# A Fourier mixer and a long convolution on one core: three kinds of short matmul blocks put together, and another choice of buffers and DMA-split tiles

## The chip, the core and the metric

The kernel runs on one core of a Trainium2 chip. The metric is the device time of one execution in microseconds; the kernel before took 584.09 us as the median of three runs (583.81 to 584.11). The core has five engines with a queue of their own: TensorE (PE, with the weight loads shown apart as PEld), VectorE (DVE), ScalarE (ACT), GpSimd (POOL) and SyncE (SP). Each engine takes its instructions strictly in the order in which the program lists them. Here POOL and SP only issue DMAs.

## What is computed

Two independent results stand side by side in the output:

```python
def _A_ref(x, dft_seq_re, dft_seq_im, dft_hid_re, dft_hid_im):
    a = jnp.einsum("bsd,ed->bse", x, dft_hid_re)
    b = jnp.einsum("bsd,ed->bse", x, dft_hid_im)
    return jnp.einsum("ts,bse->bte", dft_seq_re, a) - jnp.einsum("ts,bse->bte", dft_seq_im, b)

def _B_ref(u, log_A_real, A_imag, C_real, C_imag, log_dt, D_skip):
    dt = jnp.exp(log_dt)
    A = -jnp.exp(log_A_real) + 1j * A_imag
    C = (C_real + 1j * C_imag) * dt[:, None]
    P = jnp.exp((A * dt[:, None])[:, :, None] * jnp.arange(L)[None, None, :])
    K = 2.0 * jnp.einsum("dn,dnl->dl", C, P).real          # 512 channels, 128 states, 2048 taps
    y = irfft(rfft(u.T, 2 * L) * rfft(K, 2 * L), 2 * L)[:, :L].T
    return y + u * D_skip

return jnp.concatenate([_A_ref(...), _B_ref(...)], axis=-1)   # 2048 rows, 512 + 512 columns
```

All is float32. `x` and `u` have 2048 rows and 512 columns.

## The kernel before

**The first half, called the stream here.** The Fourier mixer is two chains of large matmuls (class `Fnet`). The sequence matrices S come in 8 groups (4 column blocks, real and imaginary), each of 16 tiles of 128x512; then 4 groups of 8 tiles take the results `p` back from DRAM and multiply them by the hidden matrices. To get float32 precision from the fast fp32r matmul, each tile is split into `hi` and `lo`, and each product is three matmuls (hi x hi, hi x lo, lo x hi) of 128x512 into one of four PSUM banks `acc`: 640 such triples, all at L366. A split takes one ACT instruction (L221, hi) and one DVE instruction (L225, lo), from a buffer `raw` that SP's DMA filled. There is a second way (`load_soft`): POOL issues a DMA that casts S to `hi`, ACT writes -hi into `lo` (L318), and a second DMA of POOL adds S onto it; DVE has no part in it. The table `SOFTS` says which tiles go this way: 28, four in each of groups 1 to 7. `RAWS` = 7 raw buffers and `DEPTH` = 4 pairs hi/lo hold what is ahead of PE.

**The second half, called the blocks.** The convolution (class `Ssm`) is a hand-made Fourier transform in small matmuls, each kind a block of PE work put between matmuls of the stream. All blocks write two PSUM buffers `f` of two banks each, handed out by `banks`:

- `stage1_u` (L890, 8 blocks): first step of the transform of u; results go out through ACT and two DVE instructions (L902, L904) for each buffer.
- `taps` (L801, 16 blocks): the convolution's taps K from two tables t1 and t2 that DVE builds by repeated products (L605, L614, L628, L634). This is most of DVE's work.
- `stage1_k` (L832, 8 blocks): first step of the transform of K.
- `product` (L992, 16 blocks, four in each of four quarters of the channels): second step of both transforms; ACT copies the result (L1006) and DVE forms the complex product (L1009, L1011, L1019, L1022).
- the inverse's first step, tile name `ia` (L1029, 16 blocks, four in each quarter), and its last step, tile name `ib` (L1078, 8 blocks, two in each quarter).

**What sets the order.** Nothing is scheduled on the chip. Python generators describe the work; each yields the engine, an assumed duration and an urgency, and the class `Plan` runs them like a small event simulation on the host and writes the instructions down in the order that comes out. For PE a yield also names the number of instructions, since `Plan.fetched` assumes that they are loaded in pieces of 256. So a change of an assumed duration or of a table moves instructions on every engine. `LATE` gives the urgency of the products of each quarter, `JOIN` the number of quarters whose `ia` may be put into the same block as a `taps` (class `Joined`, list `waiting`); before, `JOIN` is 0 and none is.

Of the kernel before, what the change touches and what calls it, by code (L numbers as in the profile page):

```python
# [11 lines left out]
AF = mybir.ActivationFunctionType  # L12
# [42 lines left out]
APART = None, True  # L55
LATE = 1, 1, 3, 1


def HELD():
    return 1  # L60


# [20 lines left out]
class Plan:  # L83
# [103 lines left out]
def dve(cols, rate=1.0):  # L187
    return (66 + cols / rate) / 960
# [6 lines left out]
class Fnet:  # L195
# [149 lines left out]
    def matmuls(self):  # L345
        nc = self.nc
        for g in self.groups:
            still = (self.x, self.x_ev) if g[0] == "s" else (self.w, self.w_ev)
            items, acc = self.items[g], []
            for batch in [[i] for i in items[:-BATCH]] + [items[-BATCH:]]:  # L350
                for d in range(4):
# [3 lines left out]
                    for i in batch:  # L355
# [53 lines left out]
class Joined(Event):  # L409
# [18 lines left out]
class Ssm:  # L428


    def __init__(self, tc, ctx, plan, fnet, nd, ldt, dsk, uG, f1u, f1k, w2, ia, ib, out):
# [14 lines left out]
        self.t1s, self.t2s, self.css = Sem(2), Sem(1), Sem(2)  # L446
        self.kss, self.res, self.xks = Sem(1), Sem(1), Sem(1)
        self.waiting, self.taps_left, self.pars = [], 16, Sem(1)
        self.sets, self.set_ev = {}, [Event(), Event()]
# [27 lines left out]
    def banks(self, n):  # L477
# [7 lines left out]
        self.plan.put(self.one)  # L485
        return got

    def give(self, k):
# [294 lines left out]
    def taps(self, ks, n, done):  # L783
# [4 lines left out]
        other = self.waiting.pop(0) if self.waiting else None  # L788
        got = yield from self.banks(2 if other else 1)
        k, p = got[0]  # L790
        yield "pe", 1.97 + (1.05 if other else 0), None, 320 if other else 256
        if other:
            other.run(got)
        t1, t2 = self.t1.pop(n), self.t2
# [13 lines left out]
        while self.waiting and not self.taps_left:  # L808
# [3 lines left out]
                             p[:, :, 256:].rearrange("p o (i l) -> p l o i", i=4), AF.Copy)  # L812
        if other:
            other.leave(k)
        else:
            self.give(k)
        done()

    def stage1_k(self, ks, n, ev):
# [6 lines left out]
        got = yield from self.banks(2)  # L826
        yield "pe", 1.11, None, 64
        for a in range(2):
# [50 lines left out]
    def stage1_u(self, k):  # L879
# [4 lines left out]
        got = yield from self.banks(2)  # L884
        yield "pe", 1.13, None, 32
        for r in range(2):
# [94 lines left out]
    def product(self, b, h, q, got, done):  # L981
# [22 lines left out]
        def half(r, k, p):  # L1004
            yield "act", act(1024), HELD
            a.activation(uk[:, r].rearrange("p g c n d -> p g (c n d)"), p, AF.Copy)  # L1006
            self.give(k)
            yield "dve", dve(512)
            v.tensor_tensor(P[:, r], t[:, r], u[:, r], op=OP.mult)  # L1009
            yield "dve", dve(512), *APART  # L1010
            v.tensor_tensor(t[:, r], t[:, r], u[:, r, :, ::-1], op=OP.mult)  # L1011
            left[0] -= 1
            if not left[0]:
                self.plan.set(ready)
        for r in range(2):
            self.plan.spawn(half(r, *got[r]), LATE[h])
        yield ready
        yield "dve", dve(512)
        v.tensor_tensor(u[:, :, :, 0], P[:, :, :, 0], P[:, :, :, 1], op=OP.subtract)  # L1019
# [3 lines left out]

        def run(got):
            for c, Y in enumerate((u, t)):
# [41 lines left out]
    def inverse(self, b, h, i, n):  # L1067
# [8 lines left out]
        for w in range(n // 2):  # L1076
            for y in range(2):
                nc.tensor.matmul(ps[64 * y:64 * y + 64, w // 4, PART * (w % 4):PART * (w % 4) + PART],  # L1078
                                 self.ib[:, n * i + 2 * w + y], z[:, 2 * w + y], start=True, stop=True,
                                 tile_position=(0, 64 * y))  # L1080
        o = n * i // 2
        for w in range(0, n // 2, 4):
            yield "act", act(512)
            nc.scalar.activation(z[:, w:w + 4], ps[:, w // 4].rearrange("p (w d) -> p w d", w=4), AF.Copy)
        self.give(k)
        yield "dma", load(32 * n, 270)
# [81 lines left out]
```

## Time and profile before

| what | value |
|---|---|
| median of three runs | 584.09 us |
| the profiled execution's own time | 582.56 us |
| its span, first to last instruction | 580.8 us |
| TensorE clock granted | 0.999 |
| PE blocks of the convolution by line | L890 8, L801 16, L832 8, L992 16, L1029 16, L1078 8 |
| DMA moved | 133.10 MB |

The profile gives each engine's busy time, the chain of work that ended last, groups of instructions by line, and a timeline. A matmul's row lasts longer than the distance to the next row's start, because matmuls overlap; what a block costs is read from the starts. The records count an fp32 matmul of a block twice and an fp32r matmul of the stream once, and each has a weight load beside it.

### The profile page before, as it was taken

The page shows a single profiled execution, that of the slowest core. Times are in us where ns is not written, and L with a number is a line of the kernel's source. Part 1 is how long each engine was busy: PE and PEld are TensorE (multiplying, and loading weights), DVE is VectorE, ACT ScalarE, POOL GpSimd, SP SyncE. Part 2 cuts the span into 40 slices and gives each one's busy share as a digit, 9 for nine tenths or more (in the row PEclk, how much of TensorE's full clock was granted, in tenths as well). Part 3 has the DMA queues.
Part 4 walks back from the last instruction along what each step waited for, and adds up shares of the span by engine and source line. Part 5 has one row for each costly group of instructions (what it writes and reads, how often), then busy time and mean ns, then how long its engine had stood idle before and what let it go on. Part 6 is the DMA issues. An engine that isn't in the chain of part 4 may idle for free.

```text
span 580.8 us, 15376 instructions
## 1 busy us (share of the span) xinstructions
PE 571.1 (98%) x6150; PEld 436.1 (75%) x6150; DVE 512.5 (88%) x911; ACT 371.2 (64%) x729; POOL 40.3 (7%) x60
## 2 busy tenths in 40 slices
PE   8999999999999999999999999999999999999996
PEld 6877777788777777778877777777687777776685
DVE  6999999999999999999999999999989999346410
ACT  4779665763777595768568585945588744445522
POOL 0000000000100000100000001001100000000000
PEclk9999999999999999999999999999999999999999
DMA  8999999986469767876797887479989995789564
GB/s 248 327 372 263 280 294 276 285 262 170 133 159 239 207 171 218 205 180 207 207 222 190 237 216 226 125 186 296 243 280 262 243 282 184 209 251 303 169 195 144
DMA packets 147831, 133.10 MB, mean 229 GB/s; under 512 B 47280, under 2 KB 107312, under 8 KB 147504
## 3 DMA queue, kind: packets, MB, share of 16 engines
q1 hardware_dynamic: 139408, 117.05, 66.7%
q0 software_dynamic: 8064, 14.68, 12.6%
q8 instruction: 48, 0.79, 0.6%
q10 hardware_dynamic: 288, 0.39, 0.2%
q14 instruction: 23, 0.19, 0.1%
HBM read 89.36 MB, written 42.73 MB: 227 GB/s over the span
## 4 chain that ended last, share of the span: by engine, by line
PE 70%; DVE 23%; issue 4%; DMA 2%; SPq 0%; ACT 0%; DVEq 0%; ACTq 0%
PE acc L366 55%; DVE prod L605 8%; DVE t L614 4%; PE f L992 4%; PE f L801 3%; DVE lo L225 3%; PE f L1029 3%; PE f L1078 2%; PE f L890 2%; DVE t L634 1%; PE f L832 1%; DVE z L1009 1%; DVE cs L675 1%; DMA zl<-zs 1%; DVE uk L1011 1%
## 5 line engine op out<-in xcount | busy, mean ns | idle before, releaser
L366 PE MATMUL acc<-hi,x_hi 128*128 128x512 f32 x640 | 258.2, 403 | 0.3 <-ACT hi L221 0.3
L366 PE MATMUL acc<-lo,x_hi 128*128 128x512 f32 x640 | 250.2, 391 | 0.0
L366 PE MATMUL acc<-hi,x_lo 128*128 128x512 f32 x640 | 249.7, 390 | 0.1
L605 DVE TENSOR_TENSOR prod<-t,cs 128x1024 f32<-128x1024 f32 (+4 forms) x192 | 163.1, 867 | 1.7 <-ACT t L723 0.6
L366 PEld LDWEIGHTS acc<-hi,x_hi 128*128 128x128 f32 x640 | 120.1, 188 | 49.8 <-issue 23.7
L366 PEld LDWEIGHTS acc<-hi,x_lo 128*128 128x128 f32 x640 | 120.3, 188 | 26.5 <-DVE x_lo L225 0.5
L366 PEld LDWEIGHTS acc<-lo,x_hi 128*128 128x128 f32 x640 | 120.3, 188 | 23.0 <-DVE lo L225 0.2
L221 ACT ACTIVATE hi<-raw 128x512 fp32r<-128x512 f32 x132 | 82.6, 627 | 64.0 <-PE acc L366 48.5
L225 DVE TENSOR_TENSOR lo<-raw,hi 128x512 fp32r<-128x512 f32 x132 | 90.1, 684 | 28.2 <-ACT hi L221 21.9
L614 DVE TENSOR_TENSOR t<-prod 128x512 f32<-128x512 f32 (+4 forms) x192 | 94.0, 511 | 1.0
L621 ACT ACTIVATE square<-t 128x256 f32<-128x256 f32 (+1 forms) x64 | 36.7, 573 | 31.0 <-DVE t L614 28.3
L320 POOL DMA_DIRECT2D lo<-in_sT x28 | 24.3, 868 | 214.1 <-ACT lo L318 33.8
L1006 ACT ACTIVATE uk<-f 128x1024 f32<-128x1024 f32 x32 | 31.1, 1017 | 11.8 <-PE f L992 11.8
L801 PEld LDWEIGHTS f<-t,t 128*32 128x32 f32 x2048 | 29.5, 110 | 7.9 <-issue 5.8
L801 PE MATMUL f<-t,t 128*32 128x64 f32 x2048 | 32.4, 220 | 1.9 <-issue 1.4
L389 ACT ACTIVATE y<-acc 128x512 f32<-128x512 f32 x47 | 28.0, 595 | 8.7 <-PE acc L366 8.6
L1009 DVE TENSOR_TENSOR z<-uk 128x512 f32<-128x512 f32 x32 | 21.9, 684 | 9.6 <-ACT uk L1006 7.4
L315 POOL DMA_DIRECT2D hi<-in_sT x28 | 16.2, 577 | 189.4 <-PE acc L366 147.0
L1044 ACT ACTIVATE z<-f 128x512 f32<-128x512 f32 x32 | 17.7, 592 | 13.3 <-PE f L1029 13.3
L634 DVE TENSOR_TENSOR t<-square 128x128 f32<-128x128 f32 (+1 forms) x64 | 24.6, 385 | 0.0
L992 PE MATMUL f<-xt,w 64*32 64x256 f32 x768 | 23.5, 379 | 0.0
L1011 DVE TENSOR_TENSOR uk<-uk 128x512 f32<-128x512 f32 x32 | 22.1, 690 | 0.9
(94 smaller groups left out, 490.7 us busy)
## 6 DMA issues: line engine op xcount, KB each, us to landing
raw<-in_sT SPq DMA_DIRECT2D x99, 256.0 KB, 5.4
p<-y SPq DMA_DIRECT2D x32, 256.0 KB, 3.2
xk<-xk_sb SPq DMA_DIRECT2D x32, 256.0 KB, 5.2
zs<-z SPq DMA_DIRECT2D x32, 256.0 KB, 3.3
zl<-zs SPq DMA_DIRECT2D x16, 512.0 KB, 5.0
raw<-p SPq DMA_DIRECT2D x32, 256.0 KB, 4.4
hi<-in_sT POOLq DMA_DIRECT2D x28, 256.0 KB, 4.6
lo<-in_sT POOLq DMA_DIRECT2D x28, 256.0 KB, 4.9
```

The costliest lines, as they stand in the source:

```text
L221: self.nc.scalar.activation(hi, src, AF.Copy)
L225: self.nc.vector.tensor_tensor(lo, src, hi.bitcast(F32), op=OP.subtract)
L366: nc.tensor.matmul(acc[d], l[:, cols], r, start=k == 0 and n == 0, stop=k == len(items) - 1 and n == 2)
L389: self.nc.scalar.activation(y, ps, AF.Copy, scale=-1.0 if g[2] == 1 else 1.0)
L605: self.nc.vector.tensor_tensor(p.rearrange("p k d c m -> p k (d c) m"), src.rearrange("p d c l -> p (d c) l")[:, None, :, rows].to_broadca ...
L614: self.nc.vector.tensor_tensor(dst[:, :, :, rows], p[:, 0], p[:, 1, :, ::-1], op=OP.add)
L621: self.nc.scalar.activation(sq, t[:, :, :, m // 2:m], AF.Square)
L634: self.nc.vector.tensor_tensor(t[:, :, 0, m:2 * m:2], box[0][:, :, 0], box[0][:, :, 1], op=OP.subtract)
L801: nc.tensor.matmul(ps[32 * j:32 * j + 32, i], t1[:, d, c], t2[:, d, c], start=c == 0, stop=c == 1, tile_position=(0, 32 * j))
L992: nc.tensor.matmul(got[r][1][32 * xx:32 * xx + 32, g, 256 * c:256 * c + 256], self.w2[rows, 2 * q + r, xx, 32 * c:32 * c + 32], xt[rows].r ...
L1006: a.activation(uk[:, r].rearrange("p g c n d -> p g (c n d)"), p, AF.Copy)
L1011: v.tensor_tensor(t[:, r], t[:, r], u[:, r, :, ::-1], op=OP.mult)
```

## The change

Five things change.

1. `JOIN` 0 becomes 2: an `ia` of quarters 0 and 1 waits for the next `taps` and is written into the same block, ahead of it, into the free half of the same buffers. The block then takes both buffers.
2. `WAITS` = 3 is new: an `ib` of quarters 0, 1 and 2 waits in the list `late` for a later `ia` block (or for a `taps` block, where no `ia` waits), and is written into it at columns 256 on. Its result then lies in two buffers.
3. In the products of quarters 0 to 2 the two DVE multiplications, until now made for each half as soon as it was there, are made once for both halves (`times`). `LATE` of quarter 2 goes from 3 to 1, and the urgency of these multiplications in quarter 3 is `LAST`.
4. `SOFTS` takes 30 tiles, five in each of groups 2 to 7; `RAWS` 7 becomes 5 and `DEPTH` 4 becomes 5.
5. Some assumed durations of PE blocks are other numbers, which moves instructions alone.

```diff
-LATE = 1, 1, 3, 1
+LATE = 1, 1, 1, 1
+def LAST():
+    return LATE[3]
...
-                    dur += 0.11 if stream else 0.09
+                    dur += 0.14 if stream else 0.11
...
-                        yield "pe", 0.683, None, 6
+                        yield "pe", 0.681, None, 6
...
 class Joined(Event):
-    def run(self, got, shared=True):
-        self.got, self.users = got, {k: 1 for k, _ in got}
-        if shared:
-            self.users[got[0][0]] = 2
-        self.fn(got)
+    def run(self, got, users, zone=0):
+        self.got, self.users, self.zone = got, users, zone
+        for k, _ in got:
+            users[k] = users.get(k, 0) + 1
+        self.fn(got, zone)
...
+    def ia_done(self):
+        self.ia_left -= 1
+        while len(self.late) > self.ia_left:
+            self.plan.set(self.late.pop(0))
...
     def taps(self, ks, n, done):
         other = self.waiting.pop(0) if self.waiting else None
-        got = yield from self.banks(2 if other else 1)
+        late = self.late.pop(0) if self.late and not other else None
+        got = yield from self.banks(2 if other or late else 1)
...
-        yield "pe", 1.97 + (1.05 if other else 0), None, 320 if other else 256
+        yield "pe", 1.97 + (1.05 if other else IB if late else 0), None, 320 if other or late else 256
...
     def product(self, b, h, q, got, done):
-            yield "dve", dve(512)
-            v.tensor_tensor(P[:, r], t[:, r], u[:, r], op=OP.mult)
-            yield "dve", dve(512), *APART
-            v.tensor_tensor(t[:, r], t[:, r], u[:, r, :, ::-1], op=OP.mult)
+            if h == 3:
+                yield from times(slice(r, r + 1), LAST)
...
+        def times(r, urgency=None):
+            n = 512 * (r.stop - r.start)
+            yield "dve", dve(n), urgency
+            v.tensor_tensor(P[:, r], t[:, r], u[:, r], op=OP.mult)
+            yield "dve", dve(n), urgency, True
+            v.tensor_tensor(t[:, r], t[:, r], u[:, r, :, ::-1], op=OP.mult)
...
         yield ready
+        if h < 3:
+            yield from times(slice(0, 2))
...
         if w.got is None:
+            late = self.late.pop(0) if self.late else None
             got = yield from self.banks(2)
-            yield "pe", 1.05, None, 64
-            w.run(got, False)
+            yield "pe", 1.15 + (IB if late else 0), None, 128 if late else 64
+            users = {}
+            w.run(got, users)
+            if late:
+                late.run(got, users, 256)
+                self.plan.set(late)
+            self.ia_done()
...
     def inverse(self, b, h, i, n):
-        (k, ps), = yield from self.banks(1)
-        yield "pe", 0.14 + 0.11 * n, None, 4 * n
...
+        j = Joined(self, run)
+        if h < WAITS and self.ia_left > len(self.late):
+            self.late.append(j)
+            yield j
+        if j.got is None:
+            got = yield from self.banks(1)
+            yield "pe", IB, None, 64
+            j.run(got, {})
...
-CHUNK, FIRST, JOIN = 32, 128, 0
-RAWS, DEPTH, STAGED, AHEAD = 7, 4, 4, 3
+CHUNK, FIRST, JOIN = 32, 128, 2
+RAWS, DEPTH, STAGED, AHEAD = 5, 5, 4, 3
 ISSUE = 1.0
-SOFTS = {(g, k) for g in range(1, 8) for k in (3, 7, 11, 15)}
+SOFTS = {(g, k) for g in range(2, 8) for k in (2, 5, 8, 11, 14)}
 BATCH = 2
+WAITS = 3
+IB = 0.14 + 0.11 * 16
```

What this does to the order is seen at three places. In the listings L370 is L366 of before, L816 is L801, L1050 is L1029, L1110 is L1078, L916 and L918 are L902 and L904, L615, L624 and L685 are L605, L614 and L675, and L229 is L225.

The first place is PE's queue where quarter 0 begins its inverse. Before, a `taps` block (t tables into `f`), five triples of the stream, and then `ia` alone:

```order
L801 MATMUL f_2315<-t_124,t_1803 32x64 x64
L366 MATMUL acc<-hi,x_hi_309 128x512
...
L366 MATMUL acc<-hi,x_lo_323 128x512
L1029 MATMUL f_2429<-uk,ia 64x256 x2
L1029 MATMUL f_2430<-uk,ia 64x256 x2
...
L366 MATMUL acc<-hi,x_hi_322 128x512
```

Now `ia` stands directly ahead of a later `taps`, in one of its two buffers (f_2619):

```order
L370 MATMUL acc<-hi,x_lo_141 128x512
L1050 MATMUL f_2619<-uk,ia 64x256 x2
L1050 MATMUL f_2620<-uk,ia 64x256 x2
...
L1050 MATMUL f_2620<-uk,ia 64x256 x2
L816 MATMUL f_2619<-t_124,t_2141 32x64 x64
L370 MATMUL acc<-hi,x_hi_140 128x512
L370 MATMUL acc<-lo,x_hi_140 128x512
```

All eight `ia` of quarters 0 and 1 are moved so; the stream has no matmul between the two kinds any more.

The second place is PE's queue at the inverse's last step. Before, `ib` stood between matmuls of the stream:

```order
L366 MATMUL acc<-lo,x_hi_140 128x512
L366 MATMUL acc<-hi,x_lo_141 128x512
L1078 MATMUL f_3412<-zl,ib 64x128 x16
L366 MATMUL acc<-hi,x_hi_140 128x512
L366 MATMUL acc<-lo,x_hi_140 128x512
```

Now it follows an `ia` of quarter 2, in two parts for two buffers:

```order
L370 MATMUL acc<-hi,x_lo_420 128x512
L1050 MATMUL f_5548<-uk,ia 64x256 x2
...
L1050 MATMUL f_5549<-uk,ia 64x256 x2
L1110 MATMUL f_5548<-zl,ib 64x128 x8
L1110 MATMUL f_5549<-zl,ib 64x128 x8
L370 MATMUL acc<-hi,x_hi_419 128x512
```

Five of the eight `ib` are written in this way; the last three stand alone as before. Before, one `ib` happened to follow a `taps` with no stream between them. In all, PE's queue is cut into 60 stretches of the stream now, and into 72 before.

The third place is DVE's queue ahead of the first `taps`. The buffer that the first `taps` takes comes free with one DVE instruction, the second of a `stage1_u` result. Before, that is the last row but one here, and 6 `stage1_u` blocks and 297 matmuls of the stream stand ahead of the first `taps` on PE:

```order
L675 TENSOR_TENSOR cs<-seed 128x704
L225 TENSOR_TENSOR lo<-raw,hi 128x512
...
L605 TENSOR_TENSOR prod<-t_938,cs 128x512
L902 TENSOR_TENSOR zl<-f_930,zl 128x512
L904 TENSOR_TENSOR zl<-f_930,zl 128x512
L654 SCALAR_TENSOR_TENSOR seed<-seed 128x352
```

Now all 8 `stage1_u` blocks and 348 matmuls of the stream stand ahead of it, and the DVE instruction is the third row from the end here:

```order
L615 TENSOR_TENSOR prod<-t_986,cs 128x1024
L229 TENSOR_TENSOR lo<-raw,hi 128x512
L624 TENSOR_TENSOR t_986<-prod 128x32x16
L916 TENSOR_TENSOR z<-f_1056,z 128x512
L918 TENSOR_TENSOR z<-f_1056,z 128x512
L916 TENSOR_TENSOR zl<-f_1113,zl 128x512
L918 TENSOR_TENSOR zl<-f_1113,zl 128x512
```

On DVE 25 instructions more stand ahead of that release than before: 8 splits (L229), 4 pairs of `stage1_u` results (L916 and L918), 3 table products of 1024 columns (L615), 3 sums of 512 and one of 256 columns (L624), and two short ones on the seeds (L664 and L666, which are L654 and L656 of before).

More of the change, by code (lines that the diff above doesn't have):

```diff
@@ L447, in __init__ @@
         self.kss, self.res, self.xks = Sem(1), Sem(1), Sem(1)
+        self.late, self.ia_left = [], 16
         self.waiting, self.taps_left, self.pars = [], 16, Sem(1)
@@ L812, in taps @@
                              p[:, :, 256:].rearrange("p o (i l) -> p l o i", i=4), AF.Copy)
-        if other:
-            other.leave(k)
-        else:
+        users[k] -= 1
+        if not users[k]:
             self.give(k)
@@ L826, in stage1_k @@
         got = yield from self.banks(2)
[L827 removed]
+        yield "pe", 1.06, None, 64
         for a in range(2):
@@ L1073, in inverse, with run @@
             nc.sync.dma_start(z[:, o:o + 8], self.zs[h].rearrange("s c l d -> (s c) l d")[:, n * i + o:n * i + o + 8])
-        (k, ps), = yield from self.banks(1)
-        yield "pe", 0.14 + 0.11 * n, None, 4 * n
[L1076 to L1080, printed above, removed]
-        o = n * i // 2
-        for w in range(0, n // 2, 4):
-            yield "act", act(512)
-            nc.scalar.activation(z[:, w:w + 4], ps[:, w // 4].rearrange("p (w d) -> p w d", w=4), AF.Copy)
-        self.give(k)
+        o = n * i // 2
+        def run(got, zone):
+            for w in range(n // 2):
+                for y in range(2):
+                    if len(got) == 2:
+                        to = got[w // 4][1][64 * y:64 * y + 64, w // 2 % 2, zone + PART * (w % 2):zone + PART * (w % 2 + 1)]
+                    else:
+                        to = got[0][1][64 * y:64 * y + 64, w // 4, PART * (w % 4):PART * (w % 4) + PART]
+                    nc.tensor.matmul(to, self.ib[:, n * i + 2 * w + y], z[:, 2 * w + y], start=True, stop=True,
+                                     tile_position=(0, 64 * y))
+        j = Joined(self, run)
[6 more added lines that the diff above has]
+            j.run(got, {})
+        for m in range(2):
+            yield "act", act(512)
+            to = z[:, 4 * m:4 * m + 4]
+            if len(j.got) == 2:
+                src = j.got[m][1][:, :, j.zone:j.zone + 2 * PART].rearrange("p b (w d) -> p b w d", w=2)
+                to = to.rearrange("p (b w) d -> p b w d", b=2)
+            else:
+                src = j.got[0][1][:, m].rearrange("p (w d) -> p w d", w=4)
+            nc.scalar.activation(to, src, AF.Copy)
+            if len(j.got) == 2:
+                j.leave(j.got[m][0])
+        if len(j.got) == 1:
+            j.leave(j.got[0][0])
         yield "dma", load(32 * n, 270)
```

10 lines of the change are left out of this document (7 added, 3 removed).

## The prediction, as it was put on record

> **What bounds the kernel now.** First the page's head, its busy row and the shares of the chain that ended last:
>
> ```profile
> span 580.8 us, 15376 instructions
> PE 571.1 (98%) x6150; PEld 436.1 (75%) x6150; DVE 512.5 (88%) x911; ACT 371.2 (64%) x729; POOL 40.3 (7%) x60
> PE 70%; DVE 23%; issue 4%; DMA 2%; SPq 0%; ACT 0%; DVEq 0%; ACTq 0%
> ```
>
> PE is busy almost throughout, so time can only come from what PE loses between or inside its blocks. The 23% of DVE in the chain call for a view by stage (columns: stage and length in us, busy time and count of PE, PEld, DVE, ACT and POOL, granted clock, DMA share, GB/s):
>
> ```profile
> 0.00:83.00 83.00, 80.95 (x400) 59.26 (x400) 77.23 (x150) 59.17 (x121) 4.60 (x10) 1.00 0.94 299
> 83.00:490.00 407.00, 404.25 (x4893) 312.61 (x4897) 401.19 (x709) 274.67 (x549) 35.67 (x50) 1.00 0.80 220
> 490.00:580.80 90.80, 85.92 (x873) 64.23 (x862) 34.03 (x54) 37.41 (x60) 0.00 (x0) 0.99 0.69 206
> ```
>
> The reader is to see two full engines up to 490 us: DVE has 401 of 407 us busy in the middle stage. A block put into PE's queue before DVE has its data makes PE wait; the stream's work left over then ends later. After 490 us only PE is full. The granted clock is 1.00, so it explains nothing here.
>
> **Term 1, fewer changes between stream and blocks.** Two places of the timeline, one clean block and the one pair that already stands together (columns: start, duration, engine and line):
>
> ```profile
> 487.86 0.39 PE L366 MATMUL acc<-lo,x_hi 128*128 128x512 f32 x1
> 488.09 0.39 PE L366 MATMUL acc<-hi,x_lo 128*128 128x512 f32 x1
> 488.41 1.99 PE L801 MATMUL f<-t,t 128*32 128x64 f32 x128
> 490.33 0.50 PE L366 MATMUL acc<-hi,x_hi 128*128 128x512 f32 x1
> 490.67 0.40 PE L366 MATMUL acc<-lo,x_hi 128*128 128x512 f32 x1
> ...
> 429.87 1.99 PE L801 MATMUL f<-t,t 128*32 128x64 f32 x128
> 431.79 1.97 PE L1078 MATMUL f<-zl,ib 128*64 128x128 f32 x32
> 433.69 0.50 PE L366 MATMUL acc<-hi,x_hi 128*128 128x512 f32 x1
> ```
>
> In the stream a start follows a start after 0.23 us. Into a block it is 0.32 (488.09 to 488.41), and the first matmul after it holds the next for 0.34 (490.33 to 490.67): 0.09 and 0.11, together 0.20 us for each block that stands alone. The pair without stream between shows that putting together saves all of it: the taps take 1.92 from start to start alone and 1.92 in the pair, and the inverse's last step 1.90. The order has 60 stretches of stream against 72, so 12 x 0.20 = **-2.4 us**. No row shows `ia` directly ahead of taps; the bounds are half the saving (-1.2) and a quarter more (-3.0), and I take the row of the pair.
>
> [...]
>
> **Term 2, the first taps.** The buffer of the first taps comes free with a DVE instruction (L904), and PE waited for it:
>
> ```profile
> 82.52 0.39 PE L366 MATMUL acc<-hi,x_lo 128*128 128x512 f32 x1
> 83.00 1.99 PE L801 MATMUL f<-t,t 128*32 128x64 f32 x128
> ...
> 76.59 0.68 DVE L902 TENSOR_TENSOR zl<-f,zl 128x512 f32<-128x512 f32 x1
> 77.31 0.69 DVE L904 TENSOR_TENSOR zl<-f,zl 128x512 f32<-128x512 f32 x1
> 77.92 0.88 DVE L675 TENSOR_TENSOR cs<-seed 128x704 f32<-128x704 f32 x1
> 82.16 0.69 DVE L904 TENSOR_TENSOR zl<-f,zl 128x512 f32<-128x512 f32 x1
> 82.77 0.52 DVE L654 SCALAR_TENSOR_TENSOR seed<-seed 128x352 f32<-128x352 f32 x1
> 83.20 0.42 DVE L614 TENSOR_TENSOR t<-prod 128x256 f32<-128x256 f32 x1
> 83.54 0.34 DVE L656 TENSOR_SCALAR seed<-seed 128x352 f32<-128x352 f32 x1
> 189.42 1.22 DVE L605 TENSOR_TENSOR prod<-t,cs 128x1024 f32<-128x1024 f32 x1
> 190.56 0.68 DVE L1019 TENSOR_TENSOR uk<-z 128x512 f32<-128x512 f32 x1
> ```
>
> DVE ended at 82.85 and the taps began at 83.00, 0.48 after the last matmul, not 0.32: DVE set this start. The order puts 25 more DVE instructions ahead of this release. By starts of these rows: 8 splits and 3 sums of 512 columns at 0.61 (77.31 to 77.92) are 6.7; 4 pairs L902 and L904 at 1.33 (76.59 to 77.92) 5.3; 3 products of 1024 at 1.14 (189.42 to 190.56) 3.4; the three short ones 0.43 (82.77 to 83.20), 0.34 and, its 0.34 less the overlap of the others, 0.25: 1.0. That is 16.4 us more. PE's way to that place grows by 51 matmuls of the stream and two L890 blocks:
>
> ```profile
> 28.80 1.11 PE L890 MATMUL f<-xt,f1u 32*64 32x512 f32 x16
> 29.84 0.50 PE L366 MATMUL acc<-hi,x_hi 128*128 128x512 f32 x1
> 255.18 17.27 PE acc L366 x75
> ```
>
> At 0.23 (17.27 / 75) these are 11.7, and two blocks at 1.04 and 0.20 are 2.5: 14.2. DVE comes 16.4 - 14.2 = 2.2 us later against PE. Since DVE has some air (77.23 of 83), I take **+2.1 us**, with 0 and 2.5 as bounds. Behind the waiting taps stands all of PE's queue, so this is paid in full.
>
> **Term 3, the later waits for DVE.** After the first taps PE loses at these places:
>
> ```profile
> 154.79 1.10 PE L801 MATMUL f<-t,t 128*32 128x64 f32 x64
> 156.26 1.10 PE L801 MATMUL f<-t,t 128*32 128x64 f32 x64 [0.37 <-DVE t L614]
> 157.29 0.50 PE L366 MATMUL acc<-hi,x_hi 128*128 128x512 f32 x1
> 163.63 1.12 PE L832 MATMUL f<-ks,f1k 32*64 32x256 f32 x32 [0.56 <-DVE ks L824]
> 492.60 1.12 PE L1029 MATMUL f<-uk,ia 32*64 32x256 f32 x32
> L1029 PE MATMUL f<-uk,ia 32*64 32x256 f32 x512 | 20.2, 389 | 0.3
> ```
>
> The taps at 154.79 take 2.50 where 1.92 is clean (0.58); L832 at 163.63 comes after 0.56 idle; the sixteen `ia` have 20.2 us busy against 16 x 1.12 = 17.9, 2.3 in all, which I put down to DVE as well, the last to write their operand. That is 3.4 us. Now `ia` of the first two quarters stands ahead of a taps whose tables DVE makes later than `ia`'s operand, so that wait should end; and the taps stand later in PE's queue than before, with less work on DVE: 24 pairs of 512 columns (1.22) are one of 1024 (1.14), 24 x 0.08 = 1.9, and two splits fewer are 1.2, so 3.1 us of air. I take **-3.3 us**; bounds -1.0 and -3.4. What is late next is `ia`'s result: it waits for its taps, and the inverse's last step follows it later. Its cover is the stream; without it an `ib` of 1.90 us would stand at the end.
>
> **Term 4, PE's instructions.** The largest single stop on PE is none of these:
>
> ```profile
> 405.63 1.81 PE f L801 x118
> 407.43 1.43 issue
> 408.86 0.41 PE f L801 x10
> 408.86 0.25 PEld L801 LDWEIGHTS f<-t,t 128*32 128x32 f32 x10 [1.59 <-issue]
> q8 instruction: 48, 0.79, 0.6%
> ```
>
> PE stops 1.6 us (its weight loads' idle time) within taps and waits for nothing that is shown. The instruction queue has 48 loads, and PE and PEld have 12300 records: 256 for each. Taps hold 256 records in 1.9 us, where the stream takes 256 in 29 (128 matmuls at 0.23). So the next load can come too late in a dense stretch: here PE stood from 407.43 to 408.86, 3.3 us from the taps' start. The eight new blocks hold 64 + 256 = 320 records in 1.05 + 1.92 = 3.0 us, with more than a whole load in each. Before, one of 16 taps stopped. I estimate 2.3 stops in eight: a stop needs the load's edge in the last 64 to 84 records (10 matmuls with their weights were left at 408.86) of 256, 0.25 to 0.33 each. 2.3 x 1.6 = 3.7, less the 1.6 of before: **+2.1 us**. Bounds: no stop at all, -1.6, and all eight, +11.2; one of 16 speaks for the near end.
>
> [...]
>
> **At nothing.** The DMA-split tiles: each of the two more costs POOL and the queues two loads of 256 KB and takes one split from DVE; POOL is 7% busy and the DMA share is 0.80 in that stage. ACT has one instruction a tile either way. RAWS and DEPTH only change how far ahead tiles lie; if that cover failed, a late tile costs up to its landing:
>
> ```profile
> raw<-in_sT SPq DMA_DIRECT2D x99, 256.0 KB, 5.4
> ```
>
> The end is the same, 15 matmuls of the stream behind the last `ib`.
>
> **Sum.** -2.4 + 2.1 - 3.3 + 2.1 = -1.5. The profiled execution took 582.56 (span 580.8 and 1.8 around it), so 581.1 there; the median of the runs is 1.5 above it, and 584.1 - 1.5 = **582.6 us**.
>
> **Rivals.**
>
> - *Instruction loads decide* (slower): four or more of the joined blocks stop, at 1.6 each as at 407.43. From a little over three the gain is gone; five give 8.0 - 1.6 = 6.4 for term 4, and 584.1 - 2.4 + 2.1 - 3.3 + 6.4 = 586.9; four give 585.3. For it: 320 dense records exceed one load. Against: 15 of 16 taps ran through, and so did the 320 records at 429.87. Chance 0.18, at 585.8.
> - *Loads hidden*: term 4 is -1.6, and the time 578.9. For it the same 15 taps. Chance 0.20. [...]
> [...]
> - *DVE stays the bound*: only 1.0 of term 3 goes, 584.9. For it DVE's 401 of 407 us; against it the later places of the taps. Chance 0.08.
> - *The change doesn't join*: the order shows 13 blocks joined; excluded.
>
> **Chances and range.** The forecast has 0.44, with a range of its own of 581.2 to 584.2. A measurement of this kernel tells 0.2% (1.2 us) from no change, so faster means under 582.9. Of the forecast 0.27 lie there and 0.17 within; hidden loads add 0.20 to faster; drain adds 0.10 to no change; DVE splits 0.04 and 0.04; the instruction rival adds 0.02 to no change and 0.16 to slower. Faster 0.47, same 0.33, slower 0.20. The range goes from hidden loads, 578.9, to the instruction rival, 585.8.
>
> **What would show it.** Right: PE's rows with `ia` and taps 2.9 to 3.0 us from first start to the stream and none between; the first taps starting near 99 us with DVE ending just ahead; L1029's successor without waits for L1022 in the first two quarters; two or three pieces of "issue" of 1.5 us inside taps that follow `ia`. Wrong: pieces of "issue" in more than three, PE waiting for hi or lo of the stream (fewer raw buffers), or waits for DVE that come back after 165 us.

## The result: slower by 1.6%

| kernel | median | runs | ratio to before, 95% interval |
|---|---|---|---|
| before | 583.90 us | 582.23 to 584.11 (6 runs) | |
| changed | 593.51 us | 589.27 to 595.10 (6 runs) | 1.0157 (1.0115 to 1.0198) |

The profiled execution of the changed kernel took 589.27 us, the lowest of its six. Where before has runs within 2 us, the changed kernel has them 6 us apart.

### The profile page after: what moved, and what is told of

Its sections match the earlier page's. It is cut to its first block, busy times and chain, and to the rows that moved or that the text cites. A ratio compares the mean times of both kernels' runs of the same rounds, so it can differ in the third digit from the quotient of the medians.

```text
span 587.5 us, 15343 instructions
## 1 busy us (share of the span) xinstructions
PE 572.2 (97%) x6150; PEld 438.0 (75%) x6150; DVE 510.9 (87%) x885; ACT 370.1 (63%) x729; POOL 43.4 (7%) x64
## 4 chain that ended last, share of the span: by engine, by line
PE 85%; DVE 4%; ACT 4%; DMA 3%; issue 2%; SPq 0%; DVEq 0%; ACTq 0%
PE acc L370 67%; PE f L1006 5%; PE f L816 4%; PE f L1110 3%; PE f L1050 3%; PE f L846 2%; DVE prod L615 1%; PE f L904 1%; DVE t L624 1%; DMA xt<-in_uG 1%; DMA par<-par_dram 1%; DMA xu<-zl 1%; ACT L672 1%; ACT L670 1%; ACT hi L225 0%
## 5 line engine op out<-in xcount | busy, mean ns | idle before, releaser
L370 PE MATMUL acc<-hi,x_hi 128*128 128x512 f32 x640 | 257.2, 402 | 0.5 <-ACT y L393 0.4
L370 PE MATMUL acc<-lo,x_hi 128*128 128x512 f32 x640 | 250.5, 391 | 4.4 <-issue 4.4
L370 PE MATMUL acc<-hi,x_lo 128*128 128x512 f32 x640 | 250.3, 391 | 0.0
L615 DVE TENSOR_TENSOR prod<-t,cs 128x1024 f32<-128x1024 f32 (+4 forms) x192 | 164.0, 870 | 3.8 <-ACT t L753 1.4
L370 PEld LDWEIGHTS acc<-hi,x_hi 128*128 128x128 f32 x640 | 120.3, 188 | 46.2 <-issue 19.1
L370 PEld LDWEIGHTS acc<-hi,x_lo 128*128 128x128 f32 x640 | 120.5, 188 | 31.0 <-issue 4.6
L370 PEld LDWEIGHTS acc<-lo,x_hi 128*128 128x128 f32 x640 | 120.5, 188 | 23.6 <-issue 0.3
L225 ACT ACTIVATE hi<-raw 128x512 fp32r<-128x512 f32 x130 | 80.7, 630 | 66.6 <-PE acc L370 56.7
L229 DVE TENSOR_TENSOR lo<-raw,hi 128x512 fp32r<-128x512 f32 x130 | 88.6, 686 | 23.8 <-ACT hi L225 21.8
L624 DVE TENSOR_TENSOR t<-prod 128x512 f32<-128x512 f32 (+4 forms) x192 | 94.9, 512 | 1.1
L324 POOL DMA_DIRECT2D lo<-in_sT x30 | 26.3, 877 | 177.9 <-ACT lo L322 102.1
L816 PEld LDWEIGHTS f<-t,t 128*32 128x32 f32 x2048 | 29.5, 110 | 6.8 <-ACT hi L225 1.6
L319 POOL DMA_DIRECT2D hi<-in_sT x30 | 17.4, 579 | 214.3 <-DVE zl L918 93.3
L816 PE MATMUL f<-t,t 128*32 128x64 f32 x2048 | 32.1, 220 | 0.8 <-DVE z L918 0.8
L1031 DVE TENSOR_TENSOR z<-uk 128x1024 f32<-128x1024 f32 (+1 forms) x20 | 20.2, 1008 | 10.3 <-ACT uk L1020 10.2
L1006 PE MATMUL f<-xt,w 64*32 64x256 f32 x768 | 25.8, 400 | 1.3 <-issue 1.2
L1006 PEld LDWEIGHTS f<-xt,w 64*32 64x32 f32 x768 | 14.5, 111 | 11.1 <-issue 4.8
L638 DVE SCALAR_TENSOR_TENSOR t<-t 128x128 f32<-128x128 f32 (+2 forms) x48 | 22.3, 465 | 0.3
```

The costliest lines, as they stand in the source:

```text
L225: self.nc.scalar.activation(hi, src, AF.Copy)
L229: self.nc.vector.tensor_tensor(lo, src, hi.bitcast(F32), op=OP.subtract)
L324: self.nc.gpsimd.dma_start(lo, src, accum_op=OP.add)
L370: nc.tensor.matmul(acc[d], l[:, cols], r, start=k == 0 and n == 0, stop=k == len(items) - 1 and n == 2)
L615: self.nc.vector.tensor_tensor(p.rearrange("p k d c m -> p k (d c) m"), src.rearrange("p d c l -> p (d c) l")[:, None, :, rows].to_broadca ...
L624: self.nc.vector.tensor_tensor(dst[:, :, :, rows], p[:, 0], p[:, 1, :, ::-1], op=OP.add)
```

## The profile after

The page's head, its busy row, the granted clock in 40 slices, and the shares of the chain that ended last:

```profile
span 587.5 us, 15343 instructions
PE 572.2 (97%) x6150; PEld 438.0 (75%) x6150; DVE 510.9 (87%) x885; ACT 370.1 (63%) x729; POOL 43.4 (7%) x64
PEclk9999999999999999999999997999999999999999
PE 85%; DVE 4%; ACT 4%; DMA 3%; issue 2%; SPq 0%; DVEq 0%; ACTq 0%
```

DVE has fallen from 23% of the chain to 4%: the chain now runs mostly along PE (85%). The clock has a 7 in one slice. What lies there is shown by the chain between 345 and 370 us (columns: start, us, what):

```profile
354.43 1.05 PE f L1050 x32
355.48 1.92 PE f L816 x128
357.40 0.43 PE acc L370
357.83 4.40 issue
362.22 2.29 PE acc L370 x5
364.52 3.59 PE f L1006 x64
```

`ia` and taps run in 1.05 and 1.92 us without a pause, as a block of 320 records. One matmul later PE stands for 4.40 us and waits for nothing that the trace shows. Then five matmuls of the stream take 2.29 us instead of 1.2, and a product takes 3.59 instead of 1.89. The windows of that stretch (after the names of the engines' busy times come the granted clock, the DMA share and GB/s) and the DMA queue of the loads in the eight us before it:

```profile
357.40:362.00 4.60, 0.43 (x1) 0.23 (x2) 4.53 (x7) 2.94 (x9) 0.00 (x0) 0.92 1.09 323
362.00:368.00 6.00, 5.78 (x69) 2.81 (x68) 2.89 (x8) 0.83 (x2) 0.88 (x1) 0.50 0.50 95
...
q8 instruction: 1, 0.02, 0.8%
```

After the stop TensorE runs at half clock for six us (0.50 from 362 to 368 us). From 355 to 363 us one load of instructions arrives; by its own times in the trace it lies between 359.98 and 360.95 us, and PE goes on 1.27 us after its end. The stop in the kernel before looks the same: its load ends at 407.27 us and PE goes on at 408.86. The third stop of 1 us or more that is put down to a load in these two executions (1.22 us within a product, which goes on at 303.84 us) ends 1.50 us after a load has landed at 302.34; the three end 1.27 to 1.59 us after a landing. So this one place costs twice: 4.5 us of standing (the next start comes 4.89 after the last, where 0.34 is clean) and 3.0 us of half speed.

PE's waits by line and by what ended them (us in total, times, longest), first the largest of before and then those of the changed kernel, without the 1.6 us at the start that both have:

```profile
PE f L801 <- issue: 1.4, 1, 1.4
PE f L832 <- DVE ks L824: 0.6, 1, 0.6
```

```profile
PE acc L370 <- issue: 4.4, 1, 4.4
PE f L1006 <- issue: 1.2, 1, 1.2
PE f L846 <- ACT uk L1020: 1.1, 2, 0.6
...
PE f L846 <- issue: 0.5, 1, 0.5
...
PE f L846 <- DVE ks L838: 0.2, 1, 0.2
```

The reader is to see two things: the waits without a cause (issue) have grown from 1.4 to 6.1 us, and the waits for DVE behind the first taps are nearly gone (0.2 us in all are left), but waits for ACT stand in their place.

From the distances of PE's starts the two profiled executions, whose spans lie 6.7 us apart, can be set against each other by the prediction's own terms (us, rounded):

| term | forecast | changed kernel |
|---|---|---|
| 1, changes between stream and blocks | -2.4 | -2.9 |
| 2, first taps and the blocks before them | +2.1 | +1.7 |
| 3, later waits for DVE and ACT | -3.3 | -0.4 |
| 4, loads of instructions, with the half clock | +2.1 | +8.7 |
| start | | -0.3 |
| sum | -1.5 | +6.8 |

## The experiments

Theory A: the time over the forecast comes from loads of PE's instructions that come too late in dense stretches, and from the half clock behind a long stop. Rivals: B, waits for ACT and DVE; C, the buffer tables; D, a drain inside the joined blocks, which is the author's assumption and shows in no row above; E, other DMAs alone delay the loads; F, the half clock belongs to the loads and not to idleness.

### The control, and the same order shifted against the loads

An edit in the warm-up loop alone, with 11, 20 or 27 small matmuls (44, 80, 108 records), moves every later instruction of PE against the pieces of 256. The order of the work stays the same word for word, and so does all that rivals B, C and D speak of.

```diff
             self.nc.tensor.matmul(ps[:, :256], z[:, :128], z[:, 256:], start=n == 0, stop=n == 2)
+        for n in range(27):
+            j = slice(32 * (n % 4), 32 * (n % 4) + 32)
+            self.nc.tensor.matmul(ps[j, 256:320], z[:, :32], z[:, 64:128], start=True, stop=True,
+                                  tile_position=(0, 32 * (n % 4)))
```

> The changed kernel once more, unedited, as the control of this group. Both theories: 589 to 595 us, and in the trace again a piece of issue of 4 us or more at the first ia+taps pair near 357 us with the granted clock at 0.5 for some 7 us behind it. If the long piece of issue and the half clock are missing and the time is still 589 or more, theory A (late instructions in dense blocks) is wrong.

> The changed kernel with 11 small fp32 matmuls more in the warm-up, which shift every later PE instruction by 44 records against the pieces of 256 in which they are loaded; the order of all other work is the same. Theory A (the time over the forecast comes from instructions that are loaded too late where 256 records run in less than about 5 us, and from the half clock behind a long stop): by the order the densest place now leaves 4.9 us to a load instead of 3.5, so no piece of issue over 2 us, no half clock at 362 us, two short stops of 1 to 1.8 us at most, and 581 to 584 us. Rival B (waits for ACT and DVE at the k blocks and the products decide) and rival C (fewer raw buffers): nothing changes for them, 588 to 595. Rival D (the joined blocks themselves drain): 588 to 595.

> The same with 20 small matmuls more (80 records). Theory A: by the order two dense places leave 3.2 and 3.5 us to a load, so two pieces of issue of 4 us or more, each with some 7 us of half clock behind it, and 593 to 598 us. Rivals B, C and D: the same as the changed kernel, 588 to 595.

> The changed kernel with 27 small matmuls more in the warm-up (108 records): by the order the densest places leave 5.0, 5.2 and 5.5 us to a load, and the first taps stand in the middle of a load's 256. Theory A: stops of at most 2 us at two or three places, no half clock of more than 3.4 us, 583 to 587 us, like the shift by 44. Rivals B, C and D: 588 to 595.

| shift | median | ratio to before, 95% interval |
|---|---|---|
| 0 (control) | 595.55 us | 1.0204 (1.0171 to 1.0237) |
| 44 | 585.58 us | 1.0046 (1.0021 to 1.0071) |
| 80 | 588.51 us | 1.0095 (1.0067 to 1.0124) |
| 108 | 583.27 us | 1.0009 (0.9995 to 1.0023) |

27 matmuls more make the kernel 12 us faster. None of rivals B, C and D has a place for that. The control's profiled execution (597.01 us) has three long stops. From its chain, in two pieces (`ia`, L1050, stands right ahead of both taps, L816):

```profile
101.30 3.33 issue
...
304.21 1.92 PE f L816 x128
306.13 2.29 PE acc L370 x9
308.42 1.01 PE f L1006 x28
309.43 1.95 issue
...
364.28 1.92 PE f L816 x128
366.20 0.43 PE acc L370
366.63 3.60 issue
```

Two of the three come right behind a joined pair: 320 records of `ia` and taps, 6 or 9 stream matmuls, and 128 records of a product make 460 to 466 records in some 7 us. That asks for nearly two loads of 256 in this time, and in the probe below one load came every 3.45 to 4.0 us. In the changed order 450 records stand within 8 us at seven places, in the order of before at none (counted in the two orders with the clean durations; the traces of before and of the kernel shifted by 108 show the same). In the first profile of the changed kernel five of the seven ran through, and the other two are where it stopped, near 303 and 357 us. The stop at 101 us is none of the seven: it lies within the first taps, which follow no `ia`. It was not in the first profile of this kernel, and of the two profiled executions the one with it is the slower. That may be why the runs lie 6 us apart; two profiles do not show it.

With 44 records of shift the place at 357 us runs through, at full clock. The same three blocks there (start, duration), and the windows:

```profile
355.13 1.12 PE L1054 MATMUL f<-uk,ia 32*64 32x256 f32 x32
356.18 1.99 PE L820 MATMUL f<-t,t 128*32 128x64 f32 x128
359.69 1.96 PE L1010 MATMUL f<-xt,w 64*32 64x256 f32 x64
...
357.00:368.00 11.00, 11.00 (x183) 8.55 (x172) 10.79 (x20) 8.44 (x20) 0.88 (x1) 1.00 0.97 261
```

The expectation for 108 came true, those for 44 and 80 did not: 44 was to give 581 to 584 us, and 80 was to be the worst of all with 593 to 598, but took 7 us less than the control. Its profile has two stops of 2.1 and 2.0 us, each ahead of the last one or two matmuls of a joined taps, with 3.4 us of half clock behind. So that stops come and go with the shift is shown; the place and the length of the next one could be told from the order only in part. How long after PE's progress a load lands is not constant (0.4 us after the start of the first taps in the first profile of the changed kernel, 98.9 against 98.56, and 3.7 us in the control's, 103.1 against 99.43), and what makes it so is not in the trace.

### The two prices measured by themselves

> A kernel of its own that computes none of the reference (its outputs are zeros). First, 80 matmuls of the stream's kind seven times, and ahead of each a chain of 2 to 9 dependent DVE additions of 512 columns, so that PE is idle for about 1.5 to 6 us; then 1280 matmuls of the taps' kind (2560 records, ten loads of 256) with no other DMA, and the same once more while SP loads 64 tiles of 256 KB. Theory A, from the runs so far (idle of 1.46 us and less was followed by full clock, of 1.95 and more by half clock for 3.4 or 6.8 us): behind every idle time of 2 us and more the granted clock is 0.5 for 3.4 or 6.8 us, and none behind 1.5. In the dense parts PE stops at each load, since 256 records take 1.92 us there: one load every 3.5 to 4.5 us, with and without other DMAs. Rival E (loads are late only when other DMAs hold the engines): no stop in the part without DMAs, stops only in the second. Rival F (the half clock belongs to the late loads, not to idleness): no half clock behind DVE's idle times.

First part, PE's timeline (80 matmuls and the idle time ahead of them) and two windows behind the waits (the clock is the third number from the end):

```profile
60.41 18.43 PE L79 MATMUL acc<-hi,lo 128*128 128x512 f32 x80 [1.51 <-DVE lo L94]
81.07 19.99 PE L79 MATMUL acc<-hi,lo 128*128 128x512 f32 x80 [2.23 <-DVE lo L94]
...
177.46 21.21 PE L79 MATMUL acc<-hi,lo 128*128 128x512 f32 x80 [5.14 <-DVE lo L94]
```

```profile
81.02:84.43 3.41, 3.36 (x8) 2.69 (x9) 0.00 (x0) 0.00 (x0) 0.00 (x0) 0.50 0.00 0
176.60:183.40 6.80, 5.94 (x14) 4.68 (x15) 0.77 (x2) 0.00 (x0) 0.00 (x0) 0.50 0.00 0
```

After 1.51 us of idleness the 80 take 18.43 us, at full clock; after 2.23 us they take 1.6 us more, with half clock for 3.41 us; after 5.14 us 2.8 more, with half clock for twice that. No load is late there, so rival F falls. Of the seven idle times, the one of 1.51 us was followed by full clock, and behind the six from 2.23 to 6.59 us the 80 take 1.6 to 2.8 us more.

Second part, dense matmuls without any other DMA, and the same while 64 tiles arrive:

```profile
265.49 2.04 PE L85 MATMUL f<-z 128*32 128x64 f32 x128 [1.69 <-issue]
269.22 2.04 PE L85 MATMUL f<-z 128*32 128x64 f32 x128 [1.69 <-issue]
```

```profile
384.64 3.57 PE L85 MATMUL f<-z 128*32 128x64 f32 x128 [3.06 <-issue]
...
394.84 3.53 PE L85 MATMUL f<-z 128*32 128x64 f32 x128 [4.16 <-issue]
```

128 matmuls with their weights are 256 records, and behind each 256 PE stands: one piece in 3.73 us (265.49 to 269.22), where its work takes 2.04. That is without other DMAs, so rival E falls; with them stops of 3.06 and 4.16 us come in, and half clock behind them (3.5 us for the same 128). The expectation counted ten loads; there are twenty on the instruction queue from 256 to 342 us, since each of these matmuls has two records and two of weights (5120 in all).

### One part undone

JOIN back to 0, WAITS back to 0, and the three buffer tables exchanged between the two kernels:

```diff
-CHUNK, FIRST, JOIN = 32, 128, 2
+CHUNK, FIRST, JOIN = 32, 128, 0
```

```diff
-WAITS = 3
+WAITS = 0
```

```diff
-RAWS, DEPTH, STAGED, AHEAD = 7, 4, 4, 3
+RAWS, DEPTH, STAGED, AHEAD = 5, 5, 4, 3
...
-SOFTS = {(g, k) for g in range(1, 8) for k in (3, 7, 11, 15)}
+SOFTS = {(g, k) for g in range(2, 8) for k in (2, 5, 8, 11, 14)}
```

> The changed kernel without one of its parts: ia of quarters 0 and 1 are no longer put into the block of a taps (JOIN 0), ib still wait for a later ia. 65 stretches of the stream. Theory A: the densest place leaves 4.3 us to a load, so one or two stops of 1 to 2 us, no half clock, and 583 to 587 us. Rival D (joined blocks drain): the ia+taps blocks are gone, so 582 to 585. Rival B: the waits of DVE at ia come back (2.5 us) and those for ACT stay, 588 to 594. Rival C (fewer raw buffers): nothing changes, 588 to 595.

> The changed kernel without one of its parts: ib no longer wait for a later ia (WAITS 0); ia still go with taps. 65 stretches of the stream. By the order the place that stopped at 357 leaves more than 7 us to its load now, and two places leave 4.9. Theory A: no long stop with half clock at 357 to 369, stops of 1 to 2 us at two places, five switches more (1.0 us): 584 to 589 us. Rival B (ACT's and DVE's waits decide): they are the same up to 280 us, 588 to 595. Rival C (buffers): 588 to 595. Rival D (drain in joined blocks): ia+taps are still there, ib behind ia not: 587 to 593.

> The kernel before with the changed kernel's tables SOFTS, RAWS and DEPTH alone (30 DMA-split tiles from group 2 on, 5 raw buffers, 5 pairs). Theory A: 70 stretches, two places that leave 5.0 us to a load: one or two stops of 1 to 2 us, 583 to 586 us. Rival C (fewer raw buffers make the stream wait for its tiles): PE waits for hi or lo for several us in all and the time is 588 or more.

> The changed kernel with the tables SOFTS, RAWS and DEPTH of the kernel before (28 DMA-split tiles, 7 raw buffers, 4 pairs); JOIN, WAITS and the products stay as changed. The planner gives another order by it: 57 stretches, the first taps where the kernel before has them, and by that order only one place that leaves under 5 us to a load (4.9). Theory A: no half clock and one or two stops of at most 2 us; the three fewer stretches are 0.6 us and term 2 falls away (2.1), so 579.5 to 583. Rival C (the buffer tables alone cost time, as they did by 16 us in the order of before): the same, 580 to 583; against theory A it says that the changed order with its own buffers is slow by waits for hi, lo or late DMAs, which the traces of that kernel do not show. Rivals B and D (ACT's waits; joined blocks drain): 586 to 595, since both are still there.

| kernel | median | ratio to before, 95% interval |
|---|---|---|
| changed, JOIN 0 | 610.82 us | 1.0455 (1.0416 to 1.0494) |
| changed, WAITS 0 | 595.19 us | 1.0194 (1.0166 to 1.0222) |
| before, buffers of the change | 599.41 us | 1.0296 (1.0254 to 1.0339) |
| changed, buffers of before | 589.12 us | 1.0102 (1.0089 to 1.0115) |

Theory A missed all four, by 6 to 24 us over its ranges. Each table gives a whole new order, and the order brings losses of its own, so none of them is the change less one part. WAITS 0 has one long stop, 4.48 us in the first taps (behind it half clock: three matmuls of the stream take 1.58 us, where 0.80 is clean), JOIN 0, which has no joined pair, the same stop of 4.76 us and waits for late DMAs besides. The two exchanges of buffers lose at the very end. The chain of before with the change's buffers:

```profile
574.02 5.01 PE acc L366 x21
...
579.05 0.39 ACT y L382
...
579.46 0.33 SPq L383
...
579.96 4.39 DMA zl<-zs
...
584.48 5.56 PE f L1078 x49
```

In SP's queue the load of the last `ib` operand (`zl`) stands behind the DMA of the stream's last result (L383), which waits for the stream's last matmul. So the stream is finished, PE stands for 5.5 us, and the last two `ib` take 5.56 us instead of 3.8, part of it at half clock by the author's reading (the execution's mean clock is 0.992). Rival C's number came true, but its mechanism is the smaller part: PE's waits for hi or lo are 4.3 us in all there, the exposed end is about 10. In the changed kernel neither the one nor the other is seen. Its buffers as such are neither cleared nor blamed by these runs.

### The kernel before, shifted

The same lines in the warm-up of the kernel before, with 51 and 22 matmuls (204 and 88 records).

> The kernel before with 51 small fp32 matmuls more in the warm-up, which shift every later PE instruction by 204 records; by the order the densest place then leaves 5.9 us to a load instead of 5.0. Theory A: the stop of 1.43 us in the taps at 407 goes and no other over 1 us comes, so 1 to 2 us less than the kernel before, less what the longer warm-up costs at the start (0 to 1.5 us): 580.8 to 583 us. Rivals B, C and D say nothing of it: the same as the kernel before, 582 to 584.

> The kernel before with 22 small fp32 matmuls more in the warm-up (88 records): by its order the worst place for it, four dense places that leave 4.3, 4.4, 4.9 and 5.2 us to a load. Theory A: two to four stops of 1 to 3 us, half clock behind one or two of them, 585 to 592 us, though the order of the work is that of before word for word. Rivals B, C and D: the same as the kernel before, 582 to 584.

They took 583.55 us (1.0010, 0.9989 to 1.0031) and 583.58 us (1.0014, 0.9999 to 1.0029): no difference. Theory A missed both: the first was to be 1 to 2 us faster, and the second was to be slow. In the second's profile the stops without a cause are 1.2 us in all. The first's profile, of one of its slower executions (586.01 us), has a long stop all the same, in the first taps (L805 is L801 there):

```profile
87.84 1.07 PE L805 MATMUL f<-t,t 128*32 128x64 f32 x28 [2.76 <-issue]
```

Half clock for 3.41 us follows it. So a long stop in the first taps needs no joined pair and is not the change's own. By the median the order of before still stands both shifts that were tried, and the changed order only one place of four. That fits the count of dense places above, seven against none; it is not a proof of it.

### Why term 3 did not come

In the changed kernel PE waits at two k blocks for ACT. ACT's rows at the first one (the square waits for DVE, and the second copy `uk` stands behind it), and PE's row there, after its first 8 matmuls:

```profile
225.12 0.63 ACT L631 ACTIVATE square<-t 128x512 f32<-128x512 f32 x1 [0.30 <-DVE t L624]
225.66 1.00 ACT L1020 ACTIVATE uk<-f 128x1024 f32<-128x1024 f32 x1
```

```profile
226.71 1.09 PE L846 MATMUL f<-ks,f1k 32*64 32x256 f32 x24 [0.60 <-ACT uk L1020]
```

The first try gave these copies another urgency, with the shift that looked best for the order that came out:

```diff
 def HELD():
-    return 1
+    return -1
```

> The changed kernel with ACT's copies of the products' and ia's results put ahead of its squares (urgency of those copies -1 instead of 1), and 28 small matmuls in the warm-up, the shift that by the order leaves the least to load late (4.9, 5.0, 5.0 and 5.2 us). Theory A with the waits for ACT of 1.2 us at the two k blocks as a further term: those two waits go (2.4 us), the first taps run through, three short stops and no half clock: 581 to 585. If the waits for ACT are not ended, 584 to 588. Rival B (ACT's waits decide all): under 582. Rival D: 588 to 595.

It took 591.09 us (1.0137, 1.0120 to 1.0154). The waits for ACT at the k blocks were gone, as theory A had it, but the time missed its 581 to 585: the new order again had a load of `zl` behind the stream's last result, and PE waited for it for 2.9 us at the end, with half clock besides (the last 16 matmul records take 2.00 us, where 64 before them take 3.90). So a second try left the order alone and moved six instructions of ACT only, in the kernel with 27 matmuls: `run_late` writes down a held instruction right behind the copy that it is to follow.

```diff
+        def do():
+            self.nc.scalar.activation(sq, t[:, :, :, m // 2:m], AF.Square)
+            box.append(sq)
+        if self.plan.squares in SQUARES:
+            self.plan.late.append(do)
+        else:
+            do()
...
             a.activation(uk[:, r].rearrange("p g c n d -> p g (c n d)"), p, AF.Copy)
+            self.plan.run_late()
```

> The changed kernel shifted by 108 records once more, unedited, as the control for the next one on the same chip: 582.5 to 584.5 us, as the kernel before, with PE waiting for ACT for about 2.2 us at 329 us and 0.5 to 1.2 us at the k block near 281.

> The same with six instructions of ACT moved, and nothing else: at five places the copy of a product's second half stands ahead of ACT's square instead of behind it, and the last copy of the stream's group that ends near 329 us stands ahead of the Sin with its table load instead of behind it. If ACT's order is what took the place of the removed waits for DVE (term 3 failed there): the waits of 2.2 us at 329 and 1.2 us at 281 become under 0.7 and under 0.3, and the time is 579.5 to 581.5 us, 2 to 3 us under its control. Rival (DVE is the bound and gives the gain back later): the two waits go, but as much comes back as waits for DVE later or as work left at the end, and the time is within 1 us of its control.

The control took 584.15 us (1.0016, 0.9999 to 1.0034), the other 583.50 us (1.0011, 0.9997 to 1.0025). PE's waits of the control and of the kernel with the moved instructions:

```profile
PE acc L374 <- ACT y L397: 2.2, 1, 2.2
...
PE f L850 <- ACT uk L1024: 0.8, 2, 0.5
```

```profile
PE f L1029 <- ACT z L1095: 2.7, 6, 0.7
PE acc L379 <- ACT y L402: 0.7, 1, 0.7
PE f L1074 <- DVE uk L1064: 0.6, 1, 0.6
```

The two waits shrank as expected (0.7 us of the 2.2 are left), and six others came, ahead of products (L1029, L1006 in the changed kernel) that need both buffers `f` right behind a joined pair, while ACT still copies `ia`'s result `z` out of them. The rival of this experiment holds in its size, within 1 us of its control, though the waits that came back are for ACT and not for DVE. PE's waits were not removed but moved.

## Why the prediction was wrong, point by point

**Term 1 was right.** -2.9 us in the changed kernel and -2.6 in the kernel shifted by 108, against -2.4. The row at 355.48 has the taps 1.92 us behind `ia` with nothing lost between. The drain to which the chances give 0.10, time lost at each change of tile shape, was the author's assumption and no run shows it: taps (128x32) take the clean 1.92 us there right behind `ia` (32x64).

**Term 2 was right in size**, +1.7 and, shifted by 108, +1.9. Its place was right in part. PE does wait for DVE at the first taps:

```profile
98.56 2.14 PE L816 MATMUL f<-t,t 128*32 128x64 f32 x128 [0.84 <-DVE z L918]
```

But that start loses 0.9 us where before it lost 0.16, so 0.7 of the 1.7 lie there. The rest lies in the `stage1_u` blocks ahead, where the prediction had put no wait.

**Term 3 failed.** The waits for DVE went as predicted: `ia` shows 17.9 us without idle time,

```profile
L1050 PE MATMUL f<-uk,ia 32*64 32x256 f32 x512 | 17.9, 387 | 0.0
```

and its 2.3 us of before are gone. The step that failed is "that wait should end", taken as a gain. PE met ACT's queue a little later instead, for 3.7 us against 4.1 of such waits before, and 4.4 in the kernel shifted by 108. So the term gave -0.4 us, not -3.3. The rival in which DVE stays the bound had the size better (1.0 of term 3), though ACT is the engine named: its copies stand in order behind squares that wait for DVE.

**Term 4 failed, and it decides.** Its mechanism was the right one and was named as a rival (four or more stops at 1.6 each), but the term was mis-sized, +2.1 us against +8.7, in three steps. "At 1.6 each as at 407.43": the long stops took 3.3 to 4.4 us in the two profiles of the changed kernel. Half clock was not in the price at all, though 3.41 us of it cost 1.6 us in the probe and the place at 362 us lost 3.0 us by it; "the granted clock is 1.00, so it explains nothing here" held for the execution of before that was read, whose longest stop is 1.43 us, and not for what longer stops bring. And the count looked at the 320 records of a joined block, where the product behind it makes them 466: in these two profiles no long stop lies inside a joined block, but in each of them two stops lie behind one. Shifted by 108 the same term is +0.1, and the sum of all terms -0.3: with the loads out of the way the change is worth nothing that can be measured (1.0009).

**At nothing** held for POOL and the DMA-split tiles: PE's waits for hi and lo do not show among those of the changed kernel. Of the signs against it that the prediction named, the waits that come back after 165 us came for ACT instead of DVE. Pieces of issue were three in the first profile, where more than three were named, and four in the control's. Of the signs for it, the pieces of issue inside taps that follow `ia` did not come in either profile.

## What to carry to other kernels

Putting blocks of short instructions side by side had a price here that no single block shows (4.5 us of standing and 3.0 us of half speed behind one joined pair): count the instructions per microsecond over a whole load (256 records here), through the blocks that follow, and not over the block that was joined. An idle time of TensorE like those here (2.23 us and more in the probe, 1.95 us in the control) is to be priced with the half clock that may follow it (3.41 us of it cost 1.6 us behind the 2.23). And an order that a planner writes cannot be undone part by part; an edit that leaves the order alone and shifts it, or moves single instructions, tells the causes apart.

## What the runs showed of the hardware that was not expected

- The half clock came after less idleness than it lasted (3.41 us of it behind 2.23 us in the probe), and not always. Behind 1.95 us of idleness the control had half clock (35 records of the product take 2.12 us, where 64 take 1.89), behind 1.97 us the probe's dense part had none (128 records in 2.04 us, as behind the next stops of 1.69). In the two profiles of the kernel shifted by 108, PE waits 2.2 us for the same copy near 331 us; behind it one has the full clock and the other half:

```profile
331.65:335.05 3.40, 3.40 (x44) 2.46 (x50) 2.76 (x5) 3.40 (x10) 0.00 (x0) 1.00 0.38 127
```

```profile
331.65:335.05 3.40, 3.40 (x9) 2.65 (x8) 2.73 (x5) 3.40 (x10) 0.00 (x0) 0.50 0.38 125
```

- With the DMA engines otherwise idle, loads of 256 records came every 3.45 to 4.0 us in a row in the probe, and never faster; 44 records of place in the program were worth 10 us (595.55 against 585.58).
- Open: why a load of instructions sometimes starts late. At the first taps it was in time in one execution of the changed kernel (landed at 98.9 us) and 3.3 us late in another (landed at 103.1); the DMA share was 1.04 and 1.01 there in the two, so the load on the queues does not tell them apart.
